# Attention with an expert layer on one core: three pieces of work moved in the expert part's written order

## The chip, the cores and the metric

The kernel runs on one core of a Trainium2 chip. The metric is device time of one execution, in microseconds (us), lower is better. The engines are called as in the profile: PE (TensorE products; PEld its weight loads), DVE (VectorE), ACT (ScalarE), POOL (GpSimd), SP (SyncE, which issues transfers); SPq and POOLq are their queues.

## The reference, cut to what matters

```python
# attention: 8 batches x 8 heads, 576 positions, 64 wide, block-causal (blocks of 64)
scores = q @ k.T / 8, masked where the key's block is later than the query's
attn = softmax(scores);  out = attn @ v          # x = out as [4608 rows, 512]
# expert layer: 8 experts, each row goes to one of them
logits = x @ w_gate + modality_bias[modality_id]
e = argmax(logits);  gate = softmax(logits)[e]
for each expert e, for its rows:  h = relu(x @ w1[e])          # 512 -> 1024
                                  out = gate * (h @ w2[e])     # 1024 -> 512
```

## The kernel before, in words

**Attention.** 32 pairs of heads go through a pipeline of slots, one pair per slot. The order of all work within a slot is a list written by hand (`ORDER`; `LAST` for the last slot, 32), and the program order on each engine is that order. `EARLY_STEPS` hangs first steps of the expert layer at places in slots 30 and 31: `ids` loads row numbers, `fetch` gathers 128 rows twice by POOL, `stage` lets SP load a weight chunk (512 KB) into one of two buffers `raw`, `cast00` to `cast02` let POOL's queue load the first three chunks rounded to the PE's format, and `lowerp` makes on POOL what the rounding left over (`L897`, chunk minus rounded chunk) and stages the next chunk. In each slot `vh` splits the values of a pair: ACT rounds (`L262`) and POOL subtracts (`L263`, tile `vhl`); the products `X`, `Y`, `W` of that pair (`L422`) need both.

**Routing.** After the last batch its rows' places are worked out (`routing`), POOL scatters row numbers into five blocks of `idlist` in memory (`L576`), and every expert's rows are then found there as a run of numbers.

**Experts.** `run_all` works through segments of rows in a fixed order: three of 256 rows for the fullest expert "a" (`n` is the segment's number; `n` = 0 is begun in the attention's last slot), three of 512 for "a" (`n` = 3 to 5), four of 512 for the second expert "b", one of 256 for a third expert "c" chosen on the chip, and a last one of 128 for "b" (`parts` = 1). What is left after these would run in a loop that tests its count on the chip. A segment of 256 rows takes: four up products (`up`, 24 products each, `L1007`) into one of three banks `s`, each followed by ACT's relu (`L1013`) and DVE's remainder (`L1014`); the next segment's rows brought into columns (`plain_rows`, ACT `L952`, and `turn_rows`, PE `L991`; or, for gathered quarters, `flip_rows`, DVE `L959`, and `split_rows`, `L969`, `L970`); and two halves of down products (`down`, 24 each, `L1053`), each given out by ACT's scaling (`L1086`) and a scatter of POOL (`L1087`). Segments from `n` = 3 on are gathered in quarters of rows, 16 gathers (`L940`) for 512 rows, eight of them issued in `n` = 1 and eight in `n` = 2. The numbers of the quarters come from `spread`: ACT multiplies row numbers by four (`L918`, tile `plain`), DVE copies and adds (`L920`, `L922`, tile `sub`). `load_ids` (`L909`, `L910`) reads a row out of a register's tile and lets POOL load that run of `idlist`; `next_segment` (DVE, 11 small instructions from `L1098`) chooses the third segment's expert, `trips` (to `L1112`) counts what is left. The last segment's up products (`up_few`, 24 products `L1029`) write `scratch` after relu (ACT `L1031`, DVE `L1033`); `turn_few` transposes that (`L1040`) and splits it (ACT `L1042`, DVE `L1043`).

Ahead of the loop over segments stand, in this order:

```python
idsa = self.load_ids(sel["rr"], 0, COVER - LEAD, "a")
idsb = self.load_ids(sel["rb"], 0, COVER_B, "b")
suba = self.spread(idsa, "a")
self.next_segment("c")
...
subb, subc = self.spread(idsb, "b"), self.spread(idsc, "c")
```

Of the kernel before, what the change touches and what calls it, by code (L numbers as in the profile page):

```python
# [14 lines left out]
I32 = mybir.dt.int32  # L15
AF = mybir.ActivationFunctionType
ALU = mybir.AluOpType
AX = mybir.AxisListType
ET = mybir.EngineType
# [4 lines left out]
N, DM, NE, DF = 4608, 512, 8, 1024  # L24
NPAIR = B * H // 2
PPB = H // 2
XW = 512
Z = 4
IW = 16
SLOT = 256  # L30
NSLOT = 9
FEW = 128
REGION = N + SLOT
NROW = NE * REGION
# [38 lines left out]

EARLY_STEPS = {
    (NPAIR - 2, "SA2"): ("stage", "ids", "cast00"),
    (NPAIR - 2, "ZB"): ("fetch", "stage", "cast01", "cast02", "lowerp"),
    (NPAIR - 1, "q1"): ("lowerp", "lowerp"),
    (NPAIR - 1, "ZB"): ("fetch",),
}
# [712 lines left out]
class Experts:  # L792
# [110 lines left out]
        self.nc.scalar.copy(self.target(k, name, c)[0], st)  # L903
        self.lower(on_pool)

    def load_ids(self, rowi, first, n, name, eng=ET.Pool, most=(NE - 1) * REGION):
        nc = self.nc
        ids = self.cst.tile([128, n // 128, 2], I32, name=f"ids_{name}")
        r = nc.values_load(rowi[0:1, 0:1], engines={eng}, min_val=0, max_val=most, skip_runtime_bounds_check_because="a row of an expert's own region")  # L909
        (nc.sync if eng == ET.SP else nc.gpsimd).dma_start(ids, self.idlist[bass.ds(r + first, n), 0:2].rearrange("(p a) o -> p a o", p=128))  # L910
        return ids

    def spread(self, ids, name):
        nc, n = self.nc, ids.shape[1]
        plain = self.cst.tile([128, n], F32, name=f"plain_{name}")
        lines = self.cst.tile([32, n, Z], F32, name=f"lines_{name}")
        sub = self.cst.tile([128, n, Z], I32, name=f"sub_{name}")
        nc.scalar.mul(plain, ids[:, :, 0], float(Z))  # L918
        for g in range(Z):
            nc.vector.tensor_copy(lines[:, :, g], plain[32 * g : 32 * g + 32])  # L920
        for z in range(Z):
            nc.vector.tensor_scalar(sub[32 * z : 32 * z + 32], lines, float(z), None, ALU.add)  # L922
        return sub

    def fetch(self, ids, t, name, nrows=N, parts=2, sub=None):
        s = Pair()
# [92 lines left out]
        self.up_relu(s)  # L1019

    def up_few(self, s):
        nc = self.nc
        wh, wl = self.w[s.name, 0]
        for f in range(2):
            fs = slice(512 * f, 512 * f + 512)
            hp = self.bank("s")
            mm = [(x, kc, w) for kc in range(4) for x, w in ((s.xh, wh), (s.xh, wl), (s.xl, wh))]
            for i, (x, kc, w) in enumerate(mm):
                nc.tensor.matmul(hp, self.x(x, kc, 128), w[:, kc, fs], start=i == 0, stop=i == len(mm) - 1)  # L1029
            if f == 0:  # L1030
                nc.scalar.activation(self.scratch[:, fs], hp, AF.Relu)  # L1031
            else:
                nc.vector.tensor_scalar(self.scratch[:, fs], hp, 0.0, None, ALU.max)  # L1033

    def turn_few(self, s, f):
        nc = self.nc
        x = self.bank("s")
        for a in range(4):
            m = 128 * (4 * f + a)
            nc.tensor.transpose(x[:, 128 * a : 128 * a + 128], self.scratch[:, m : m + 128], self.idf)  # L1040
        hh, hl = (t.rearrange("p a t -> p (a t)") for t in self.next_hidden())
        nc.scalar.copy(hh, x)  # L1042
        nc.vector.tensor_tensor(hl, x, hh, ALU.subtract)  # L1043
        s.hs += [(hh[:, 128 * a : 128 * a + 128], hl[:, 128 * a : 128 * a + 128]) for a in range(4)]
# [70 lines left out]
    def run_all(self, steps):  # L1115
        tc, ctx, nc, cst, sel, plan = self.tc, self.ctx, self.nc, self.cst, self.sel, self.plan
        dve = nc.vector
        self.wk = wk = ctx.enter_context(tc.tile_pool(name="wk", bufs=1, side="right", reuse_waits="tile"))
        self.w["b", 0] = [wk.tile([128, 4, DF], F32R, name=f"w0{x}b") for x in "hl"]
        w2 = [wk.tile([128, 2, DM], F32R, name=f"w1b{i}") for i in range(5)]  # L1120
        self.xl = [wk.tile([128, 512], F32R, name=f"xl{i}") for i in range(3)] + [self.xlast]
        self.o1 = self.ps_o.tile([128, 512], F32, name="o1")
        sb = [self.ps_s.tile([128, 512], F32, name="s") for _ in range(3)]
        self.sb, self.tb = sb, [self.ps_t.tile([128, 512], F32, name="t") for _ in range(2)]
        self.ys = [self.o0, self.o1, self.bbank, sb[2]]
        self.w["b", 1] = [w2[0:4], w2[4:5] + self.low2]
        s = self.parts[0]
        flat = self.xg[1]
        self.parts.append(self.fetch(*plan[2]))
        self.down(s, 0, range(6))  # L1130
        for f in steps[0:13]:
            f()
        self.down(s, 1, range(6))
        for f in steps[13:]:
            f()
        self.flush()
        for i in range(2):
            self.down(s, i, range(6, 8))
        self.rem, left = (cst.tile([128, NE], F32, name=n) for n in ("rem", "left"))
        self.rowc, self.expc = (cst.tile([128, 1], I32, name=n) for n in ("rowc", "expc"))  # L1140
        idsa = self.load_ids(sel["rr"], 0, COVER - LEAD, "a")
        idsb = self.load_ids(sel["rb"], 0, COVER_B, "b")
        suba = self.spread(idsa, "a")
        self.next_segment("c")
        sel["ec"] = self.expc
        idsc = self.load_ids(self.rowc, 0, SLOT, "c", most=NROW - SLOT)
        dve.tensor_tensor(left, self.run, sel["start"], ALU.subtract)
        self.more = self.trips(left)
        subb, subc = self.spread(idsb, "b"), self.spread(idsc, "c")

        wide = (COVER - LEAD) // 512
        plan += [(idsa, 4 * t, "a", N, 4, suba) for t in range(wide)]
        plan += [(idsb, 4 * t, "b", N, 4, subb) for t in range(COVER_B // 512)]
        plan += [(idsc, 0, "a", N, 2, subc), (idsb, 2 * NSLOT - 2, "b", N, 1, subb)]
        segs = self.parts + [self.fetch(*x) for x in plan[NLEAD:]] + [None]
        for n in range(1, len(plan)):
            s, nxt = segs[n : n + 2]
            ahead = segs[max(n + 1, NLEAD)]

            def follow(part):  # L1160
                if nxt is None:
                    return
                if nxt.sub is not None:
                    self.split_rows(nxt, part)
                elif part == 0:
                    self.turn_rows(nxt)

            if s.parts == 4:
                self.sb = sb[0:2]
                for m in range(8):  # L1170
                    self.up_wide(s, m)
                    self.give_owed()
                    if m > 1:
                        self.down_wide(s, m - 2)
                    self.gather(ahead, 3)
                    if m in (2, 5) and self.staged:
                        self.convert(n < NLEAD + wide)
                    if m == 6:
                        self.flip_rows(nxt)
                follow(0)  # L1180
                self.down_wide(s, 6)
                follow(1)
                self.down_wide(s, 7)
            else:
                if s.parts == 1:
                    self.up_few(s)
                    self.turn_few(s, 0)
                    self.turn_few(s, 1)
                    self.hturn += 2
                else:  # L1190
                    for m2 in range(4):
                        self.up(s, m2)
                        self.give_owed()
                        self.gather(ahead, 2)
                        if m2 == 1 and n < NLEAD:
                            self.convert(True)
                        if m2 == 2 and nxt.sub is None:
                            self.plain_rows(nxt, flat)
                if nxt and nxt.sub is not None:
                    self.flip_rows(nxt)  # L1200
                follow(0)
                self.down(s, 0)
                follow(1)
                if s.parts == 2:
                    self.down(s, 1)
        assert not self.staged and not self.owed

# [95 lines left out]
```

## Time and profile before

| | us |
|---|---|
| median of three runs (lowest, highest) | 832.88 (831.9, 835.57) |
| the profiled execution | 832.91 |
| its span, first to last instruction | 831.3 |
| PE busy in the span | 801.5 (96%) |
| DVE, ACT, POOL busy | 466.1, 465.3, 550.6 |
| mean granted PE clock | 0.984 of full speed |

A busy share of 96% is a mean over stages. What PE still waits for, and where its clock is not the full one, says what can be had; the rows below are read for that. The profiled execution's time lies 1.6 us over its span and 0.03 us over the median.

### The profile page before, as it was taken

The page shows a single profiled execution, that of the slowest core. Times are in us where ns is not written, and L with a number is a line of the kernel's source. Part 1 is how long each engine was busy: PE and PEld are TensorE (multiplying, and loading weights), DVE is VectorE, ACT ScalarE, POOL GpSimd, SP SyncE. Part 2 cuts the span into 40 slices and gives each one's busy share as a digit, 9 for nine tenths or more (in the row PEclk, how much of TensorE's full clock was granted, in tenths as well). Part 3 has the DMA queues.
Part 4 walks back from the last instruction along what each step waited for, and adds up shares of the span by engine and source line. Part 5 has one row for each costly group of instructions (what it writes and reads, how often), then busy time and mean ns, then how long its engine had stood idle before and what let it go on. Part 6 is the DMA issues. An engine that isn't in the chain of part 4 may idle for free.

```text
span 831.3 us, 15373 instructions
## 1 busy us (share of the span) xinstructions
PE 801.5 (96%) x5027; PEld 717.7 (86%) x5027; DVE 466.1 (56%) x1695; ACT 465.3 (56%) x1384; POOL 550.6 (66%) x399
## 2 busy tenths in 40 slices
PE   7999999999999999998949999999999999999995
PEld 5999999999999999998948888888888888888884
DVE  5889999999999999995631313131223213231220
ACT  6999999999999998996412312222131313222221
POOL 6998789898999999968355572655645362714030
PEclk9999999999999999999988999999999999999998
DMA  8887877767786768676611221221222131211010
GB/s 256 244 259 214 243 214 223 234 190 237 213 266 189 241 184 271 185 201 174 230 32 61 77 76 39 75 76 70 82 85 67 47 104 42 85 51 42 21 51 22
DMA packets 64306, 117.91 MB, mean 142 GB/s; under 512 B 18761, under 2 KB 31929, under 8 KB 64216
## 3 DMA queue, kind: packets, MB, share of 16 engines
q1 hardware_dynamic: 53600, 96.00, 38.6%
q0 software_dynamic: 10624, 20.89, 7.9%
q8 instruction: 41, 0.67, 0.3%
q14 instruction: 41, 0.34, 0.1%
HBM read 77.21 MB, written 21.95 MB: 119 GB/s over the span
## 4 chain that ended last, share of the span: by engine, by line
PE 40%; issue 34%; POOL 16%; DVE 4%; DMA 3%; ACT 1%; POOLq 1%; SPq 0%; DVEq 0%
PE o L422 11%; POOL xr L940 11%; PE b L441 6%; PE s L286 5%; PE s L287 4%; PE t L345 3%; POOL out L1087 3%; PE t L350 2%; PE s L278 2%; PE t L331 1%; PE t L363 1%; DVE scratch L291 1%; PE s L279 1%; DMA xrows<-xr 1%; DVE ptl L382 1%
## 5 line engine op out<-in xcount | busy, mean ns | idle before, releaser
L382 DVE TENSOR_TENSOR ptl<-t,pth 128x512 fp32r<-128x512 f32 (+3 forms) x288 | 140.1, 505 | 16.4 <-ACT pth L375 14.0
L291 DVE TENSOR_SCALAR_CACHE_REDUCE scratch<-s 128x128 bf16<-128x128 f32 (+4 forms) x288 | 132.6, 478 | 9.2 <-PE s L287 6.4
L319 ACT ACTIVATE pm<-s,nm 128x256 f32<-128x256 f32 (+3 forms) x256 | 134.8, 535 | 5.2 <-DVE scratch L291 4.6
L375 ACT CAST pth<-t 128x512 fp32r<-128x512 f32 (+3 forms) x288 | 122.8, 453 | 16.1 <-PE t L345 10.7
L422 PE MATMUL o<-pth,vhl 128*128 128x320 f32 (+3 forms) x384 | 110.6, 306 | 2.7 <-POOL vhl L263 2.5
L422 PE MATMUL o<-ptl,vhl 128*128 128x320 f32 (+3 forms) x384 | 110.8, 308 | 0.0
L286 PE MATMUL s<-qkt 128*128 128x256 f32 (+3 forms) x256 | 89.9, 364 | 1.4 <-DVE qkt L238 1.4
L215 POOL TENSOR_TENSOR qkt<-rawq,qkt 64x1280 fp32r<-64x1280 f32 x30 | 87.7, 2925 | 2.4
L211 POOL TENSOR_TENSOR z<-raw,qkt 64x1152 fp32r<-64x1152 f32 x30 | 79.8, 2659 | 13.3 <-issue 8.3
L940 POOL DMA_INDIRECT xr<-xrows,sub_b x68 | 69.8, 1027 | 20.6 <-issue 20.3
L1087 POOL DMA_INDIRECT out<-scratch,ids_b x17 | 17.0, 1002 | 98.8 <-ACT scratch L1086 84.5
L287 PE MATMUL s<-z 68*128 68x256 f32 (+3 forms) x256 | 80.0, 325 | 1.2 <-DMA z<-cm 1.2
L422 PEld LDWEIGHTS o<-pth,vhl 128*128 128x128 f32 x384 | 73.1, 190 | 4.7 <-POOL vhl L263 2.8
L1065 ACT ACTIVATE qkt<-s 128x512 fp32r<-128x512 f32 x28 | 16.8, 599 | 103.8 <-PE s L1063 103.8
L1065 ACT ACTIVATE ptl<-s 128x512 fp32r<-128x512 f32 x28 | 16.8, 599 | 102.8 <-PE s L1063 102.8
L422 PEld LDWEIGHTS o<-ptl,vhl 128*128 128x128 f32 x384 | 73.2, 191 | 1.3
L441 PE MATMUL b<-bk,ot 128*128 128x72 f32 x512 | 64.7, 269 | 0.5 <-DVE ei_a L97 0.3
L441 PEld LDWEIGHTS b<-bk,ot 128*128 128x128 f32 x512 | 64.2, 192 | 0.9 <-ACT ott L434 0.9
L1066 DVE SCALAR_TENSOR_TENSOR qkt<-s,qkt 128x512 fp32r<-128x512 f32 x14 | 9.7, 692 | 86.9 <-ACT qkt L1065 86.9
L940 POOL DMA_INDIRECT xr<-xrows,sub_a x48 | 48.3, 1006 | 14.0 <-issue 13.4
L319 ACT ACTIVATION_READ_ACCUMULATOR pm<-s,nm 128x1 f32 x256 | 53.2, 208 | 0.0
L286 PEld LDWEIGHTS s<-qkt 128*128 128x128 f32 x256 | 49.2, 192 | 2.5 <-DVE qkt L238 1.6
(372 smaller groups left out, 2210.5 us busy)
## 6 DMA issues: line engine op xcount, KB each, us to landing
raw<-qk SPq DMA_DIRECT2D x30, 640.0 KB, 4.3
rawq<-qk SPq DMA_DIRECT2D x30, 640.0 KB, 5.0
raw<-w SPq DMA_DIRECT2D x23, 512.0 KB, 3.5
vrt<-vr SPq DMA_DIRECT2D x32, 320.0 KB, 5.2
k2t<-z SPq DMA_DIRECT2D x64, 144.0 KB, 4.8
xrows<-xr SPq DMA_DIRECT2D x8, 1024.0 KB, 8.9
z<-qkt SPq DMA_DIRECT2D x30, 256.0 KB, 5.3
idlist<-xr SPq DMA_DIRECT2D x8, 304.0 KB, 4.1
```

The lines of the kernel that those rows point to most:

```text
L211: pool.tensor_tensor(d.k2[0:64], k, d.k[0:64], ALU.subtract)
L215: pool.tensor_tensor(d.q[0:64], q, d.q[0:64], ALU.subtract)
L286: pe.matmul(o, d.q[:, h, qs], d.k[:, h, 0:n], start=True, stop=False)
L287: pe.matmul(o, d.q2[0:68, h, qs], d.k2[0:68, h, 0:n], start=False, stop=True)
L291: dve.tensor_scalar(jks[jturn[0] % 4][:, 0 : s.shape[-1]], s, -SCALE, start, ALU.mult, ALU.min, accum_out=o)
L319: act.activation(d.pm[h][:, CHUNK_OFF[c] : CHUNK_OFF[c] + n], s[:, 256 * i : 256 * i + n], AF.Exp, bias=d.nm[:, h, c : c + 1], scale=SCALE ...
L375: act.copy(dst[0], s)
L382: dve.tensor_tensor(dst[1], s, dst[0], ALU.subtract)
L422: pe.matmul(o, w, r, start=part != "W" and i == 0, stop=part != "Y" and i == len(mm) - 1)
L441: pe.matmul(d.b[h][:, 72 * c : 72 * c + 72], d.ot[h][:, 128 * c : 128 * c + 128], w, start=True, stop=True)
L940: s.gathers.append(lambda to=to, at=at: gather(to, None, quarters, bass.IndirectOffsetOnAxis(ap=at, axis=0), bounds_check=Z * nrows - 1, o ...
L1087: last = nc.gpsimd.indirect_dma_start(self.out, bass.IndirectOffsetOnAxis(ap=s.ids[:, s.t + i, 0:1], axis=0), yo, None, bounds_check=N - 1 ...
```

## The change

Three things move; no instruction's size changes.

- At the end of slot 30 the remainder of the first weight chunk (`lowerp`) and the second `stage` stand ahead of the two gathers and the two rounding loads.
- `spread` of "a" and "b" and "c", and the choice of the third segment with its load (`third`), are taken out of the place ahead of the loop and put behind up products of `n` = 1 and `n` = 2 (`chores`); in `n` = 1 the gathers behind the four up products are 0, 2, 3, 3 instead of 2 each.
- The last segment's up products stand between the fourth and fifth of eight steps of the second down half of segment "c", and their relu goes to the row buffer `rows[1]` instead of `scratch`.

```diff
-    (NPAIR - 2, "ZB"): ("fetch", "stage", "cast01", "cast02", "lowerp"),
+    (NPAIR - 2, "ZB"): ("stage", "lowerp", "fetch", "cast01", "cast02"),
...
-        nc = self.nc
+        nc, wide = self.nc, self.rows[1]
...
             if f == 0:
-                nc.scalar.activation(self.scratch[:, fs], hp, AF.Relu)
+                nc.scalar.activation(wide[:, fs], hp, AF.Relu)
             else:
-                nc.vector.tensor_scalar(self.scratch[:, fs], hp, 0.0, None, ALU.max)
+                nc.vector.tensor_scalar(wide[:, fs], hp, 0.0, None, ALU.max)
...
-        suba = self.spread(idsa, "a")
-        self.next_segment("c")
-        sel["ec"] = self.expc
-        idsc = self.load_ids(self.rowc, 0, SLOT, "c", most=NROW - SLOT)
-        dve.tensor_tensor(left, self.run, sel["start"], ALU.subtract)
-        self.more = self.trips(left)
-        subb, subc = self.spread(idsb, "b"), self.spread(idsc, "c")
+        def third():
+            self.next_segment("c")
+            sel["ec"] = self.expc
+            self.load_ids(self.rowc, 0, SLOT, "c", most=NROW - SLOT, ids=idsc)
+            dve.tensor_tensor(left, self.run, sel["start"], ALU.subtract)
+            self.more = self.trips(left)
+        chores = {
+            (1, 1): lambda: self.spread(idsa, suba, "a"),
+            (1, 3): third,
+            (2, 0): lambda: self.spread(idsb, subb, "b"),
+            (2, 2): lambda: self.spread(idsc, subc, "c"),
+        }
...
-                    self.up_few(s)
                     self.turn_few(s, 0)
                     self.turn_few(s, 1)
...
                         self.give_owed()
-                        self.gather(ahead, 2)
+                        chores.get((n, m2), lambda: None)()
+                        self.gather(ahead, (0, 2, 3, 3)[m2] if n == 1 else 2)
...
-                if s.parts == 2:
+                if nxt and nxt.parts == 1:
+                    self.down(s, 1, range(4))
+                    self.up_few(nxt)
+                    self.down(s, 1, range(4, 8))
+                elif s.parts == 2:
                     self.down(s, 1)
```

In the rows of the program order below, lines of the changed kernel are mostly one lower than before (`L1013` is `L1012`).

On POOL at the end of slot 30 (`qkt_110` is the first weight chunk, `xr_114` the gathered rows, `vhl` the last pair's values), before:

```order
L263 TENSOR_TENSOR vhl<-vrt,vhl 128x10x64
L936 DMA xr_114<-xrows,ids_lead 128x512 x2
L892 ISA
L892 DMA qkt_108<-w 128x4x256
L892 ISA
L892 DMA z_102<-w 128x4x256
L897 TENSOR_TENSOR qkt_110<-raw_111,qkt_110 128x1024
L263 TENSOR_TENSOR vhl<-vrt,vhl 128x10x64
```

and now, where the remainder `L897` has gone from just ahead of the second `vhl` to just ahead of the gathers:

```order
L263 TENSOR_TENSOR vhl<-vrt,vhl 128x10x64
L897 TENSOR_TENSOR qkt_110<-raw_111,qkt_110 128x1024
L935 DMA xr_114<-xrows,ids_lead 128x512 x2
L892 ISA
L892 DMA qkt_108<-w 128x4x256
L892 ISA
L892 DMA z_102<-w 128x4x256
L263 TENSOR_TENSOR vhl<-vrt,vhl 128x10x64
```

On ACT at the start of `n` = 1 (the scalings of `n` = 0, then this segment's relus), before:

```order
L1086 ACTIVATE scratch<-o_6861,ids_lead 128x512
L918 ACTIVATE plain_a<-ids_a 128x12
L918 ACTIVATE plain_b<-ids_b 128x17
L918 ACTIVATE plain_c<-ids_c 128x2
L1013 ACTIVATE qkt_110<-s 128x512
L1013 ACTIVATE qkt_109<-s 128x512
L903 CAST w0hb<-raw_112 128x4x256
L1013 ACTIVATE ptl_104<-s 128x512
L952 COPY xr_114<-xr_114 128x512 x2
L1013 ACTIVATE ptl_104<-s 128x512
```

and now, with two relus ahead of `plain_a`, and `plain_b` and `plain_c` gone to `n` = 2:

```order
L1085 ACTIVATE scratch<-o_6861,ids_lead 128x512
L1012 ACTIVATE qkt_110<-s 128x512
L1012 ACTIVATE qkt_109<-s 128x512
L918 ACTIVATE plain_a<-ids_a 128x12
L903 CAST w0hb<-raw_112 128x4x256
L1012 ACTIVATE ptl_104<-s 128x512
L951 COPY xr_114<-xr_114 128x512 x2
L1012 ACTIVATE ptl_104<-s 128x512
```

On ACT at the end of the kernel (segment "c" given out, then the last segment), now; before, the relu `L1031` stood behind both scalings of `ids_c`:

```order
L1085 ACTIVATE scratch<-o_98,ids_c 128x512
L1030 ACTIVATE xr_115<-s 128x512
L1085 ACTIVATE scratch<-o_6861,ids_c 128x512
L1041 CAST qkt_110<-s 128x512
L1041 CAST qkt_109<-s 128x512
L1085 ACTIVATE scratch<-o_98,ids_b 128x512
```

The second scaling of "c" now stands directly ahead of the last segment's first cast.

## Rows read from the trace of the kernel before

**Rows 1.** PE's waits over the span: who waited <- for whom: us, times, longest.
```profile
PE s L1007 <- DVE qkt L1014: 11.8, 1, 11.8
PE o L422 <- POOL vhl L263: 2.5, 1, 2.5
PE s L1040 <- DVE scratch L1033: 0.4, 1, 0.4
```

**Rows 2.** Timeline around n = 1: start, us, engine, line [idle before <- releaser].
```profile
416.92 5.91 PE L1007 MATMUL s<-z,qkt 128*128 128x256 f32 x48
...
424.85 1.08 POOL L910 DMA_DIRECT2D ids_a<-idlist  x1
...
428.15 0.21 ACT L918 ACTIVATE plain_a<-ids_a 128x12 f32<-128x12 int32 x1 [10.34 <-DMA ids_a<-idlist]
...
429.14 0.75 DVE L922 TENSOR_SCALAR sub_a<-lines_a 32x48 int32<-32x48 f32 x4
...
432.70 0.15 DVE L1112 CAST counti<-count 128x1 int32<-128x1 f32 x1
...
433.75 1.08 POOL L940 DMA_INDIRECT xr<-xrows,sub_a  x1 [0.30 <-DVE lines_b L920]
...
435.89 1.04 ACT L903 CAST w0hb<-raw 128x1024 fp32r<-128x1024 f32 x1
...
437.31 1.15 ACT L952 COPY xr<-xr 128x512 f32<-128x512 f32 x2
...
437.46 5.35 PE L1007 MATMUL s<-z,qkt 128*128 128x256 f32 x24 [11.75 <-DVE qkt L1014]
```

**Rows 3.** Windows, PE alone: stretch, us, busy, granted clock, DMA share, GB/s.
```profile
384.00:385.00 1.00, 0.85 (x5) 0.74 0.93 236
387.00:388.00 1.00, 1.00 (x6) 0.55 0.04 8
...
428.00:429.00 1.00, 0.00 (x0) 0.93 0.53 17
...
442.00:443.00 1.00, 1.00 (x9) 0.75 0.50 120
```

**Rows 4.** Timelines of POOL, ACT and PE at the end of the attention.
```profile
376.18 1.10 POOL L936 DMA_INDIRECT xr<-xrows,ids_lead  x1 [8.03 <-DVE scratch L291]
...
380.16 2.44 POOL L897 TENSOR_TENSOR qkt<-raw,qkt 128x1024 fp32r<-128x1024 f32 x1
...
382.09 1.17 ACT L952 COPY pm<-xr 128x512 f32<-128x512 f32 x2
...
382.47 1.62 POOL L263 TENSOR_TENSOR vhl<-vrt,vhl 128x640 fp32r<-128x640 f32 x1
...
384.14 0.39 PE L422 MATMUL o<-pth,vhl 128*128 128x256 f32 x1 [2.52 <-POOL vhl L263]
...
384.80 1.08 PE L991 MATMUL t<-cf,pm 128*128 128x128 f32 x4
...
388.36 0.88 PE L1007 MATMUL s<-z,qkt 128*128 128x256 f32 x6
```

**Rows 5.** Chain (start, us, what), 375 to 475; then landings of chunk loads, 364 to 384.
```profile
368.37 6.91 DMA xrows<-xr
...
DMA to landing us min/median/max: 4.6/5.2/5.8
```

**Rows 6.** Timelines of POOL, DVE and PE from the last gather of n = 2 to n = 3.
```profile
468.63 1.00 POOL L940 DMA_INDIRECT xr<-xrows,sub_a  x1 [0.30 <-issue]
...
472.78 1.29 DVE L970 TENSOR_TENSOR xl<-xr,z 128x512 fp32r<-128x512 f32 x2 [0.73 <-ACT z L969]
...
476.98 0.39 PE L1063 MATMUL s<-z,qkt 128*128 128x512 f32 x1
```

**Rows 7.** Timeline of the last segment.
```profile
809.95 0.69 ACT L1086 ACTIVATE scratch<-o,ids_c 128x512 f32<-128x512 f32 x1 [4.85 <-PE o L1053]
...
815.30 0.60 PE L1040 MATMUL s<-cf,scratch 128*128 128x128 f32 x4
```

More of the change, by code (lines that the diff above doesn't have):

```diff
@@ L904, in convert, with load_ids @@
         self.lower(on_pool)
-    def load_ids(self, rowi, first, n, name, eng=ET.Pool, most=(NE - 1) * REGION):
+    def load_ids(self, rowi, first, n, name, eng=ET.Pool, most=(NE - 1) * REGION, ids=None):
         nc = self.nc
-        ids = self.cst.tile([128, n // 128, 2], I32, name=f"ids_{name}")
+        if ids is None:
+            ids = self.cst.tile([128, n // 128, 2], I32, name=f"ids_{name}")
         r = nc.values_load(rowi[0:1, 0:1], engines={eng}, min_val=0, max_val=most, skip_runtime_bounds_check_because="a row of an expert's own region")
@@ L911, in load_ids, with spread @@
         return ids
-    def spread(self, ids, name):
+    def spread(self, ids, sub, name):
         nc, n = self.nc, ids.shape[1]
@@ L916, in spread @@
         lines = self.cst.tile([32, n, Z], F32, name=f"lines_{name}")
-        sub = self.cst.tile([128, n, Z], I32, name=f"sub_{name}")
         nc.scalar.mul(plain, ids[:, :, 0], float(Z))
@@ L922, in spread @@
             nc.vector.tensor_scalar(sub[32 * z : 32 * z + 32], lines, float(z), None, ALU.add)
-        return sub
     def fetch(self, ids, t, name, nrows=N, parts=2, sub=None):
@@ L1039, in turn_few @@
             m = 128 * (4 * f + a)
-            nc.tensor.transpose(x[:, 128 * a : 128 * a + 128], self.scratch[:, m : m + 128], self.idf)
+            nc.tensor.transpose(x[:, 128 * a : 128 * a + 128], self.rows[1][:, m : m + 128], self.idf)
         hh, hl = (t.rearrange("p a t -> p (a t)") for t in self.next_hidden())
@@ L1142, in run_all @@
         idsb = self.load_ids(sel["rb"], 0, COVER_B, "b")
-        suba = self.spread(idsa, "a")
-        self.next_segment("c")
-        sel["ec"] = self.expc
-        idsc = self.load_ids(self.rowc, 0, SLOT, "c", most=NROW - SLOT)
-        dve.tensor_tensor(left, self.run, sel["start"], ALU.subtract)
-        self.more = self.trips(left)
-        subb, subc = self.spread(idsb, "b"), self.spread(idsc, "c")
+        idsc = cst.tile([128, SLOT // 128, 2], I32, name="ids_c")
+        suba, subb, subc = (cst.tile([128, x.shape[1], Z], I32, name=f"sub_{n}") for x, n in ((idsa, "a"), (idsb, "b"), (idsc, "c")))
+        def third():
[10 more added lines that the diff above has]
+        }
         wide = (COVER - LEAD) // 512
```

## The prediction

> **What bounds the kernel now.** I read the waits of PE first, since the page's busy shares say that PE works nearly all the time. Over the span PE has two waits that count and one small one [rows 1]: 11.8 us for DVE's remainder of an up product, 2.5 us for POOL's `vhl`, 0.4 us in the last segment. Everything else in the expert part is PE behind PE, so time moves only where one of these waits moves, where PE's clock moves, or where a new wait opens.
>
> Then the timeline around the long wait [rows 2]. PE runs three groups of up products of `n` = 1 (each half of 5.91, so 2.95 us) and stops at 425.71, because the fourth needs a bank that ACT and DVE have not emptied. They have not, since ahead of the relus in ACT's order stands the multiplication of `ids_a`, and that load lands only at 428.15 (issued at 424.85). Behind it DVE works through spreads and the third segment's choice until 432.85, and ACT meets `plain_c`, before a relu is reached. PE goes on at 437.46, and then with a group of 24 products in 5.35 us instead of 2.95.
>
> [...]
>
> Last the end of the attention [rows 4]. POOL stands for 8.03 us until 376.18, then gathers, starts two rounding loads, makes the remainder (2.44 us from 380.16), and only then `vhl`, for which PE waits until 384.14.
>
> **First part: remainder ahead of the gathers.** What the gathers wait for is the store of the same buffer, 6.91 us from 368.37 [rows 5], so the wait stays. The remainder needs its rounding load, which takes at most 5.8 us to land [rows 5]. It is issued ahead of the slot's own `vhl` of 1.6 us, which ended when POOL went idle at 368.15, so by 366.6, and is there by 372.4. Then the remainder runs until about 374.9, inside the 8.03 us in which POOL has nothing to do. Gathers keep their time, `vhl` starts 2.44 us earlier and ends near 381.7, when PE arrives. PE is next late for the plain copies of the gathered rows: ACT ends them at 383.26 (382.09 + 1.17, [rows 4]), and PE's transposes, at 384.80 before, can start at 383.3. From there to the first up group took 3.56 us (to 388.36), 3.1 of them at half clock; with two waits below 1 us the clock should stay, so 2.0. That makes 385.3, a gain of 3.0 us. But later chunks' loads hang on POOL's remainders, which move by 2.44 only. I take 2.6. Bounds: 0 if the remainder isn't covered, 3.1 if nothing later holds. Of the transfers moved, the next chunk's load is issued near 375 instead of 382.6, in front of the gathers; were they delayed by it, the plain copies would be, and PE one for one.
>
> **Second part: the chores.** Now two relus precede the wait for `ids_a`, so the fourth up group finds its bank empty and PE runs until 428.66 (425.71 + 2.95). Queued behind the wait on ACT are the weight cast, the third relu, the copies of the next segment's rows and the fourth relu; PE's next work, the transposes, needs the copies. From the cast's start to the copies' end took 2.57 us (435.89 to 438.46, [rows 2]); put behind `plain_a` (428.15 + 0.21) that is 430.93. So PE waits 2.3 us where it waited 11.75. On DVE the two remaining low halves queue behind the spread, which ends at 429.9; they are needed at the down products, behind the transposes. The third choice and count took from 429.9 to 432.85, 2.95 us, and run after the fourth low half, until about 435; behind them stand the next segment's low rows, needed only by the first up group of `n` = 2, 48 down products on. They are covered, and so are the later spreads, four copies and four additions each, between up groups of 2.95 us.
>
> Whether the clock falls for a wait of 2.3 us the trace doesn't say outright: it fell for 2.52, and in the last tenths of a microsecond of it PE was already at work [rows 3, 4]. I take a fall, at 1.7 us. Before: 11.75 + (5.35 - 2.95) = 14.15. After: 2.3 + 1.7 = 4.0. Gain 10.15 us, with 8.5 as the lower bound (the copies 1 us later, and a slow stretch that costs 2.4 as in the long wait) and 11.85 as the upper (no fall).
>
> [...] The sum would be 1.7 us smaller in time without the fall.
>
> POOL has to keep up, since PE comes to `n` = 3 ten us sooner. Sixteen gathers (1.30 us each with the 0.30 between, [rows 6]), two remainders (2.44), one id load (1.08, [rows 2]) and two scatters at the gathers' cost are 16 x 1.3 + 4.9 + 1.1 + 2.6 = 29.4 us from 429.9, when `sub_a` is ready. That ends near 459.5, or 460.2 with a wait for the second scaling: the last gather starts near 458.9. Before, the first pair of rows for `n` = 3 was ready 4.8 us after the last gather's start (472.78 + 0.65 against 468.63) and PE wanted it at 476.98, 3.5 us later. Now it is ready at 463.7; PE, 10.15 us sooner, wants it at 466.8. The slack stays at 3 us; a delay of POOL costs nothing up to there.
>
> [...] The spreads now stand among the gathers. [...]
>
> **Third part: the last up products.** PE's 24 products move, none goes. What they could gain is the 0.41 us that the transposes waited for DVE's relu [rows 1]. Against that, the second scaling of "c", 0.69 us, now stands on ACT between the last product and the cast of the transposed rows, while the transposes take 0.60 [rows 7]. The cast starts up to 0.69 later, at best not at all; I take 0.3 us lost. PE's first down products need that cast and DVE's part behind it, so the 0.41 is not regained. Bounds -0.4 and +0.7.
>
> **Sum.** Against the profiled time, 832.91, which is the median but for 0.03: - 2.6 - 10.15 + 0.3 = 820.5 us, 1.5% faster.
>
> **Rivals.**
> No slow stretch in `n` = 1: 820.5 - 1.7 = 818.8. For it, the wait is shorter than any for which the trace shows a fall; against it, how near the 2.52 lies.
> The first part pays nothing: the rounding load lands later than 373.7 (376.18 less 2.44), or the copies are late behind the earlier chunk. 823.1. Against it, 5.8 us as the longest landing.
> [...]
> The wait only changes its place, and the kernel is slower: ACT stands for `ids_a` inside `n` = 1, and everything for PE's transposes is behind it. If the load landed X us later than 428.15, PE would wait X more; from X = 12.4 the kernel is no faster, and at 17 it is 4.6 us slower, 837.5. The load took 3.3 us, and nothing in its neighbourhood takes five times that.
> The change doesn't do what it says in its third part: that is in the sum.
>
> **How the numbers follow.** Likeliest, 820.5: 0.46. No slow stretch, 818.8: 0.22. First part nothing, 823.1: 0.14. POOL at `n` = 3, 822.5: 0.09. Several of these losses with another slow stretch, 825 to 829: 0.07. The ids late: 0.02. The runs before spread from 1 us below to 2.7 above their median, so the range is 817 to 826, which leaves out the last two cases and little else. A measurement of this kernel can tell about 0.5%, 4.2 us, from no change: faster means below 828.7. All but the last two cases lie below; of the last but one most does. Faster 0.94, same 0.04, slower 0.02.
>
> **What would show it.** Of PE's waits the 11.8 us for DVE's remainder goes, and one of 2 to 2.6 us for ACT's copies `L951` comes, near 426 of the new span. The clock falls there for about 3.4 us, or not at all. PE's wait for `vhl` shrinks below 0.3 us, a wait of 0.5 to 1 us for the plain copies follows it, the remainder of the first chunk runs near 373, and no slow stretch follows. From `n` = 2 to the last segment PE has no wait over 0.5 us. In the last segment the first cast starts after the second scaling of "c". The prediction is wrong if PE waits at `n` = 3 for `xl`, if `ids_a` lands over 4 us after its issue, or if the POOL wait of 8 us moves to the remainder.

## The result and the profile after

| | before | after |
|---|---|---|
| median, us (lowest, highest; 4 runs each) | 834.23 (831.9, 836.78) | 821.07 (819.87, 822.0) |
| ratio, 95% interval | | 0.9841 [0.9805, 0.9877] |
| the profiled execution, us | 832.91 | 822.0 |
| its span, us | 831.3 | 820.3 |
| mean granted PE clock | 0.984 | 0.998 |

The kernel became 1.6% faster; forecast were 820.5 us and 1.5%. The time alone does not tell that forecast from three of its rivals: the interval, taken on 834.23 us, runs from 818.0 to 824.0 us, and 818.8, 822.5 and 823.1 lie in it too. The profiles have to tell. A ratio on record is not the quotient of the two medians, so that the two can give differences almost a microsecond apart; where it matters, the text says which is meant. Ratios are of the fast executions alone, which leaves out one of the twelve of the kernel with two remainders ahead: it took 1580.55 us, and why stays open.

Read as before, first PE's waits over the span after the change (who waited <- for whom: us, times, longest):

```profile
PE t L990 <- ACT xr L951: 2.0, 2, 1.8
...
PE s L287 <- DMA z<-qkt: 1.0, 2, 0.8
PE t L990 <- ACT pm L951: 0.7, 2, 0.5
...
PE o L1052 <- ACT qkt L1041: 0.4, 1, 0.4
```

The 11.8 and 2.5 us of [rows 1] are gone. The first row is what is left of the long wait, the third what lay under the short one. The second, for a transfer, is in the attention and has no counterpart in the profile before.

The timelines around `n` = 1 after the change (start, us, engine, line), against [rows 2]:

```profile
417.58 5.91 PE L1006 MATMUL s<-z,qkt 128*128 128x256 f32 x48
...
425.51 1.08 POOL L911 DMA_DIRECT2D ids_a<-idlist  x1
...
426.21 3.04 PE L1006 MATMUL s<-z,qkt 128*128 128x256 f32 x24
...
428.89 0.21 ACT L918 ACTIVATE plain_a<-ids_a 128x12 f32<-128x12 int32 x1 [4.76 <-DMA ids_a<-idlist]
...
430.43 1.12 ACT L951 COPY xr<-xr 128x512 f32<-128x512 f32 x2
...
431.09 0.33 PE L990 MATMUL t<-cf,xr 128*128 128x128 f32 x1 [1.84 <-ACT xr L951]
431.61 0.98 PE L990 MATMUL t<-cf,xr 128*128 128x128 f32 x7 [0.19 <-ACT xr L951]
```

The fourth up group runs on at 426.21, PE stops behind it, and the transposes start as soon as the first of ACT's two copies is done. The windows (us, busy of each engine, then PE's clock, DMA share, GB/s) show a full clock at both places where [rows 3] show a fall (in the profile before to 0.50 of full from 385 to 387 and from 429 to 442):

```profile
428.00:436.00 8.00, 5.97 (x35) 4.92 (x34) 5.95 (x12) 4.24 (x8) 4.61 (x4) 1.00 0.13 21
384.00:388.00 4.00, 3.27 (x26) 2.75 (x26) 2.53 (x9) 3.36 (x11) 3.50 (x4) 1.00 1.02 259
```

The end of the attention after the change, against [rows 4]:

```profile
375.61 2.39 POOL L897 TENSOR_TENSOR qkt<-raw,qkt 128x1024 fp32r<-128x1024 f32 x1 [3.00 <-DMA qkt<-w]
379.60 1.10 POOL L935 DMA_INDIRECT xr<-xrows,ids_lead  x1 [1.60 <-DVE scratch L291]
...
383.58 1.62 POOL L263 TENSOR_TENSOR vhl<-vrt,vhl 128x640 fp32r<-128x640 f32 x1
...
385.03 0.27 PE L364 MATMUL t<-cf,pm 128*128 128x128 f32 x1
385.25 0.39 PE L422 MATMUL o<-pth,vhl 128*128 128x256 f32 x1
...
386.47 0.33 PE L990 MATMUL t<-cf,pm 128*128 128x128 f32 x1 [0.54 <-ACT pm L951]
...
389.02 1.24 PE L1006 MATMUL s<-z,qkt 128*128 128x256 f32 x9
```

The remainder fills the gap ahead of the gathers, `vhl` ends at 385.20 as PE comes, and PE then waits for ACT's plain copies. The last segment, against [rows 7]:

```profile
804.18 1.04 PE L1039 MATMUL s<-cf,xr 128*128 128x128 f32 x8
...
804.43 0.69 ACT L1085 ACTIVATE scratch<-o,ids_c 128x512 f32<-128x512 f32 x1 [5.00 <-PE o L1052]
805.02 1.06 ACT L1041 CAST qkt<-s 128x512 fp32r<-128x512 f32 x2
...
805.65 2.15 PE L1052 MATMUL o<-w1b,qkt 128*128 128x512 f32 x7 [0.43 <-ACT qkt L1041]
```

The wait for DVE's relu has become one for ACT's cast, which stands behind the scaling.

**Where the time went.** I cut both spans at rows that PE executes in either kernel. From the end of the last transposes ahead of the `vhl` products (`L364`) to the first up product of `n` = 0, "stretch A": 381.62 to 388.36 before, 385.30 (385.03 + 0.27) to 389.02 after, so 6.74 and 3.72. From the first up product of `n` = 1 to that of `n` = 2, "stretch B": 37.70 before and 25.91 after (417.58 to 443.49). The first products of `n` = 2, before and after:

```profile
454.62 0.28 PE L1007 MATMUL s<-z,qkt 128*128 128x256 f32 x1
```

```profile
443.49 0.28 PE L1006 MATMUL s<-z,qkt 128*128 128x256 f32 x1
```

Between A and B both profiles take 28.56, and behind B ("stretch C") 376.68 and 376.81 to the end. Sum: -3.02 - 11.79 + 0.13 = -14.7. The span fell by 11.0 only, since everything ahead of A took 3.68 us longer. Nothing in the change stands there that could do that: in the thirteen profiles of this study that part ends anywhere from 381.45 to 387.72, and 381.45 belongs to a kernel with the whole change (the early spread, below).

### The profile page after: what moved, and what is told of

It is laid out like the page before. It is cut to its first block, busy times and chain, and to the rows that moved or that the text cites. A ratio compares the mean times of both kernels' runs of the same rounds, so it can differ in the third digit from the quotient of the medians.

```text
span 820.3 us, 15372 instructions
## 1 busy us (share of the span) xinstructions
PE 802.3 (98%) x5027; PEld 717.2 (87%) x5027; DVE 470.8 (57%) x1695; ACT 465.1 (57%) x1384; POOL 551.8 (67%) x399
## 4 chain that ended last, share of the span: by engine, by line
PE 37%; issue 34%; POOL 19%; DMA 6%; DVE 3%; ACT 1%; POOLq 1%; SPq 0%; ACTq 0%
PE o L422 11%; POOL xr L939 11%; PE b L441 5%; PE s L286 4%; PE s L287 4%; POOL out L1086 3%; PE t L345 3%; PE t L350 2%; DMA z<-qkt 2%; PE s L278 2%; PE t L331 1%; PE t L363 1%; DMA raw<-w 1%; PE s L279 1%; DMA rawq<-qk 1%
## 5 line engine op out<-in xcount | busy, mean ns | idle before, releaser
L287 PEld LDWEIGHTS s<-z 68*128 68x128 f32 x256 | 49.9, 195 | 3.2 <-issue 1.5
```

The costliest lines, as they stand in the source:

```text
L287: pe.matmul(o, d.q2[0:68, h, qs], d.k2[0:68, h, 0:n], start=False, stop=True)
```

## The experiments

The first four ran on one chip, on which the kernel before takes 842.85 us (median of 7); the next four on a second one (832.44, 9 runs); the last three on a third (835.73, 17 runs). Ratios are to the kernel before on the same chip.

**The choice and the spreads alone** (second part of the change).

```diff
-        suba = self.spread(idsa, "a")
-        self.next_segment("c")
...
+            (1, 1): lambda: self.spread(idsa, suba, "a"),
+            (1, 3): third,
+            (2, 0): lambda: self.spread(idsb, subb, "b"),
+            (2, 2): lambda: self.spread(idsc, subc, "c"),
```

> Only the spreads, the third segment's choice and the gathers' shares are moved. Three stretches of PE's timeline are compared, since whole times of unchanged code differ by some us between executions: A, from the end of the transposes ahead of the vhl wait to the first up product of the expert layer (6.74 us before, 3.72 changed); B, from the first up product of n = 1 to that of n = 2 (37.70 before, 25.91 changed); C, from there to the last instruction (376.7 before, 376.8 changed). Theory: the parts are separate, so A stays at 6.7 with its slow clock, B is 25.9, C 376.7, and the time falls by 11.8 us. Rival: B's clock stays up only because the first part spared the slow stretch 40 us earlier; then B is 27 to 28 with a fall of the clock, and the time falls by about 10.

Measured: 832.18 us, ratio 0.9877 [0.9858, 0.9896], by which 10.4 us of 842.85 are gained (10.7 between the medians). Stretch B is 25.98, with PE's wait for the copies 1.43 + 0.19 and no slow products behind it: the seven down products that follow take 1.88 us, as after the change, where the clock is 1.00. Stretch A is 3.99, although the first part of the change is missing. Why, PE's timeline shows:

```profile
364.34 0.30 PE L422 MATMUL o<-p,vhl 128*128 128x64 f32 x1 [1.26 <-DMA p<-p4l]
...
385.25 0.39 PE L422 MATMUL o<-pth,vhl 128*128 128x256 f32 x1 [1.20 <-POOL vhl L263]
```

PE had lost 1.26 us twenty microseconds earlier to a late transfer of `p4l` (32 KB, which SP's queue copies from one tile of the pair to another); POOL did not lose it, so `vhl` was that much nearer when PE came for it. The rival, that B's clock stays up only because a slow stretch in A is spared, was not put to the test, since A has none here either.

**The remainder ahead of the gathers alone** (first part).

```diff
-    (NPAIR - 2, "ZB"): ("fetch", "stage", "cast01", "cast02", "lowerp"),
+    (NPAIR - 2, "ZB"): ("stage", "lowerp", "fetch", "cast01", "cast02"),
```

> Only the remainder of the first chunk and a stage are moved ahead of the gathers. Theory: A is 3.7 us, B and C are as before (37.7 with the long wait, 376.7), and the time falls by 3.0 us. Rival: the gain is swallowed further on, since loads of later chunks move by 2.4 us only; then the stretch from the first up product to the first of n = 1 grows from 28.56 us, and the time falls by less than 2.5.

Measured: 840.74 us, ratio 0.9984 [0.9963, 1.0006]: 1.3 us by the ratio, 2.1 between the medians, not told from nothing, where the prediction had 2.6 and the expectation 3.0. In its profile the wait for `vhl` is gone and A is 3.73. So the mechanism works and the time gains less; the next runs bear on why. The sign of the rival, a longer stretch between A and B, is there as well: 30.98 instead of 28.56. But 1.93 of the 2.42 are idle time in `L1007` that the profile gives to nothing ("issue"), and the two profiles of the changed kernel, with the same order on POOL, take 28.56. So nothing shows that the remainder swallows its gain further on.

**The last up products alone** (third part; one execution).

```diff
-                    self.up_few(s)
...
+                if nxt and nxt.parts == 1:
+                    self.down(s, 1, range(4))
+                    self.up_few(nxt)
+                    self.down(s, 1, range(4, 8))
```

> Only the last segment's up products are moved into the down products of the segment ahead, and write the row buffer. Theory: PE's wait of 0.4 us goes from one place to another, and from the last product ahead of the transposes to the first down product it is 1.70 us as in the changed kernel, against 1.66 before; A and B are as before. Rival: the second scaling on ACT costs its whole 0.7 us.

Measured: 842.54 us beside 842.85. From the start of the first transposes to the first down product behind them it took 1.46 (824.23 to 825.69), 1.42 in the kernel before (815.30 to 816.72) and 1.47 after the change: 0.05 us lost, not the rival's 0.7. Its profile is worth more for the other place. PE's timeline and PE's clock (us, busy, granted clock, DMA share, GB/s):

```profile
364.79 0.30 PE L422 MATMUL o<-p,vhl 128*128 128x64 f32 x1 [1.63 <-DMA p<-p4l]
...
388.89 0.33 PE L991 MATMUL t<-cf,pm 128*128 128x128 f32 x1 [0.76 <-ACT pm L952]
```

```profile
368.00:370.00 2.00, 2.00 (x11) 0.50 0.78 219
```

Here the late transfer was followed by a granted clock of 0.50 in each of three windows from 366 to 372; PE came so late that there was no wait for `vhl` at all (A 3.72), without the first part of the change.

**The first spread and its gathers in the last step of `n` = 1.**

```diff
-            (1, 1): lambda: self.spread(idsa, suba, "a"),
-            (1, 3): third,
+            (1, 3): lambda: (self.spread(idsa, suba, "a"), self.gather(segs[NLEAD], 4), third()),
...
-                        self.gather(ahead, (0, 2, 3, 3)[m2] if n == 1 else 2)
+                        self.gather(ahead, (0, 0, 0, 4)[m2] if n == 1 else 2)
```

> The changed kernel, with the spread of a moved from behind the second up group of n = 1 to behind the fourth, and all eight gathers of n = 1 behind it. Theory: PE waits in n = 1 because the copies of the next segment's rows stand behind ACT's wait for ids_a; with that wait behind them B loses the rest of its wait and is 23.9 us, and POOL, some 1.5 us later with its gathers, still has the sixteen ready in time, so the time is 2.0 us below the changed kernel's. DVE's first instruction of the third choice, which took 3.1 us while POOL made a remainder, takes 0.2 again, since that remainder is then over. Rival: POOL's gathers become late and PE waits at n = 3 for as much as it gains; B 23.9 but C above 378.

Measured: 831.03 us, ratio 0.986 [0.9843, 0.9878]. The wait for the copies in `n` = 1 is gone, and B is 24.33. On this chip, though, PE shows waits in the expert part that the profile gives to nothing ("issue"): 7.1 us in all here, 6.6 us in the run of the remainder alone, whose largest row is

```profile
PE s L1076 <- issue: 3.1, 3, 1.2
```

They lie in up products, most of them in segments that no edit touches, so on this chip 1.5 us could not be told. Nor does the rival's sign say anything here: C is 389.69, over its 378, but 385.42 with the choice and the spreads alone on this chip. PE shows no wait for rows at `n` = 3.

**The changed kernel again**, beside the next three.

> The changed kernel as it is, so that the next three have it beside them on one chip. The parts run alone gave 0.988 (choice and rows later) and 0.998 (remainder first) of the kernel before; if parts add up, this gives 0.984 to 0.987. Theory: 11.8 us less between the first products of n=1 and of n=2, and 3.0 us less between the end of attention's last transposes and the first up product in executions in which the kernel before waits 2.5 us there. Rival: the second saving is a thing of one execution; then the ratio is 0.986 to 0.988.

Measured: 819.78 us (818.51 to 823.36), ratio 0.9854 [0.9827, 0.988]; A 3.72, B 25.86, no "issue" wait. The interval holds both forecasts.

**The changed kernel with the remainder behind the gathers again** (the first diff above, reversed).

> The changed kernel with the remainder behind the gathers again, as before. Theory (the wait for vhl is there in every execution): 2.5 to 3.0 us slower than the changed kernel, with PE's wait of 2.5 us on vhl back in the profile. Rival (the wait is there only where PE comes early; where it waits elsewhere first, 1.3 or 1.6 us for a late p4l transfer in two profiles, POOL has caught up): 0 to 1.5 us slower in the median, and a profile with a late p4l transfer shows no wait for vhl or one of about 1 us.

Measured: 820.82 us, ratio 0.986 [0.9837, 0.9883]: 1.0 us slower between the medians, not told from nothing, and in the rival's 0 to 1.5. PE's timeline:

```profile
363.34 0.30 PE L422 MATMUL o<-p,vhl 128*128 128x64 f32 x1 [0.96 <-DMA p<-p4l]
...
383.97 0.39 PE L422 MATMUL o<-pth,vhl 128*128 128x256 f32 x1 [0.92 <-POOL vhl L263]
```

A is 3.73: a wait of 0.92 for `vhl` costs nothing, since under it lies the one for the plain copies (0.76 + 0.19 in the run beside it). The second thing to see is PE's clock behind the wait in `n` = 1. First this run, whose wait there is 1.78, then the changed kernel again, with 1.79:

```profile
430.00:431.00 1.00, 1.00 (x5) 0.50 0.28 78
431.00:432.00 1.00, 1.00 (x4) 0.50 0.27 70
432.00:433.00 1.00, 1.00 (x4) 0.50 0.01 0
```

```profile
430.00:431.00 1.00, 1.00 (x7) 1.00 0.32 78
431.00:432.00 1.00, 1.00 (x6) 1.00 0.26 66
432.00:433.00 1.00, 1.00 (x6) 1.00 0.02 4
```

The same stretch of code behind the same wait, in two kernels that differ only at the end of the attention, runs at 0.50 of the full clock in one execution and at 1.00 in the other; B is 27.43 against 25.86, so the slow stretch costs 1.57. In neither is there a slow stretch in A, so a spared one does not keep B's clock up.

**The first spread one up group earlier.**

```diff
-            (1, 1): lambda: self.spread(idsa, suba, "a"),
+            (1, 0): lambda: self.spread(idsa, suba, "a"),
```

> The changed kernel with the first spread one step earlier, behind the first up product group of n=1 instead of the second, so that ScalarE waits for ids_a with two eviction copies behind it instead of one. Theory (the wait is for the landing of ids_a, 428.9 in the profile, and only what is queued behind it counts): PE stops at about 426 for 3 to 4 us instead of 2.0 at 429 to 431, so 1 to 2 us slower than the changed kernel. If a wait of this length makes the clock fall, as 2.52 us did in the kernel before, 1.7 us more: 2.7 to 3.7 us slower. Rival (the slack of PE behind that place takes it up): no difference.

Measured: 820.42 us, ratio 0.9859 [0.9834, 0.9884]. PE did not stop for 3 to 4 us at 426. The first relu still stands ahead of the spread, and its bank is the one that the fourth group takes; so the wait stays at the transposes, longer by the one relu more behind `ids_a` (0.47 from start to start):

```profile
427.67 0.33 PE L990 MATMUL t<-cf,xr 128*128 128x128 f32 x1 [2.26 <-ACT xr L951]
```

In that profile the clock fell behind it (0.57 of full from 428 to 432), and B is 27.91, of which 2.05 over 25.86 are 0.47 of wait and 1.6 of slow clock. The median moved by 0.6 us, about as much as the wait and not told from nothing; the forecast of 1 to 2 us or more fell.

**Late spread, and the last transposes inside the segment ahead.** The late spread as above, and:

```diff
-                    self.turn_few(s, 0)
-                    self.turn_few(s, 1)
...
-                    self.down(s, 1, range(4, 8))
+                    self.down(s, 1, range(4, 6))
+                    self.turn_few(nxt, 0)
+                    self.turn_few(nxt, 1)
+                    self.down(s, 1, range(6, 8))
```

> The changed kernel with the first spread and its gathers in the last step of n=1, and the last segment's two sets of transposes inside the segment ahead, between its sixth and seventh group of down products. Theory: the 2.0 us wait in n=1 goes (1.5 us less there, as one profile showed) and the 0.4 us wait ahead of the last down products goes: 1.5 to 2 us faster than the changed kernel. Rival (gathers that start 2 us later make n=3 late, or POOL's work is only moved): no faster than the changed kernel, with a new wait of PE at the start of n=3.

Measured: 816.71 us (815.83 to 818.34), ratio 0.981 [0.9789, 0.9831], 3.1 us below the changed kernel beside it, where 1.5 to 2 were forecast; its slowest execution is faster than that one's fastest. From `n` = 0 on the profile has no wait of PE but 0.9 us for the plain copies; B is 23.44. The transposes run between down products:

```profile
427.98 1.03 PE L990 MATMUL t<-cf,xr 128*128 128x128 f32 x8
...
799.25 1.04 PE L1039 MATMUL s<-cf,xr 128*128 128x128 f32 x8
```

Between the two profiles B is shorter by 2.42, of which the wait was 1.98 (1.79 + 0.19), and C by 0.68. The gathers that start later did not make `n` = 3 late.

**A second remainder ahead of `vhl`** in the kernel before.

```diff
-    (NPAIR - 2, "ZB"): ("fetch", "stage", "cast01", "cast02", "lowerp"),
-    (NPAIR - 1, "q1"): ("lowerp", "lowerp"),
+    (NPAIR - 2, "ZB"): ("fetch", "stage", "cast01", "cast02", "lowerp", "lowerp"),
+    (NPAIR - 1, "q1"): ("lowerp",),
```

> The kernel before with a second of POOL's remainders ahead of vhl (in it one stands there), so that vhl comes 2.4 us later still. Theory: PE waits for it in every execution, and the wait grows from 2.5 to 4.9 us: 2.4 us slower than the kernel before, with the stretch from the last transposes of the attention to the first up product at 9.1 us or more (6.74 before, 3.7 where nothing waits). Rival (an earlier late p4l transfer takes the wait's place in some executions): the wait in the profile is 4.9 us less what PE stood for p4l, and the median grows by 1 to 2 us.

Measured: 839.98 us, ratio 1.0046 [1.0027, 1.0065]: 3.8 us slower by the ratio, 4.25 between the medians, where 2.4, or by the rival 1 to 2, were forecast. Stretch A is 10.30, with a mean granted clock of 0.91 from 388 to 424, behind the wait. POOL and PE:

```profile
385.88 2.34 POOL L897 TENSOR_TENSOR qkt<-raw,qkt 128x1024 fp32r<-128x1024 f32 x1 [1.61 <-DMA qkt<-w]
388.18 1.53 POOL L263 TENSOR_TENSOR vhl<-vrt,vhl 128x640 fp32r<-128x640 f32 x1
...
389.77 0.58 PE L422 MATMUL o<-pth,vhl 128*128 128x256 f32 x1 [5.42 <-POOL vhl L263]
```

The second remainder brought its own wait, 1.61 for its chunk, so `vhl` came 4.0 later and not 2.4. With the 1.35 that PE stood for `p4l` in this profile, 2.52 - 1.35 + 4.0 = 5.2, near the 5.42 seen. POOL's work ahead of `vhl` does pass on to PE one for one, less what PE was late.

**The first spread ahead of `n` = 1 again**, all else as changed.

```diff
+        self.spread(idsa, suba, "a")
         chores = {
-            (1, 1): lambda: self.spread(idsa, suba, "a"),
```

> The changed kernel with the first spread back in front of the up products of n=1, the third segment's choice and the other spreads still late. Theory (the wait of 11.8 us is the landing of ids_a, and behind it the choice and the later spreads in ScalarE's and VectorE's order): about 5 us of it come back, since ScalarE stands for ids_a with all relus behind it and VectorE makes the spread (1.5 us) before the first low half; with a slow stretch of 1.7 to 2.4 us the first products of n=2 come 30.5 to 31.2 us after those of n=1 (37.7 before, 25.9 or 27.4 changed). So 0.989 to 0.992 of the kernel before. Rival one (the landing of ids_a is all of it): 37 us, no gain but the remainder's. Rival two (the choice and its load are all of it): 26 us, as the changed kernel.

Measured: 825.43 us, ratio 0.9891 [0.9859, 0.9922]; B 30.12, a little under the 30.5 to 31.2 forecast. ACT and PE:

```profile
425.83 0.21 ACT L918 ACTIVATE plain_a<-ids_a 128x12 f32<-128x12 int32 x1 [10.32 <-DMA ids_a<-idlist]
...
428.35 4.62 PE L1006 MATMUL s<-z,qkt 128*128 128x256 f32 x24 [4.95 <-DVE qkt L1013]
```

The group of 24 takes 4.62 where it takes 3.04 at full clock (0.59 of full from 428 to 432). So 4.95 of the 11.75 us are the landing of `ids_a` and its spread ahead of the relus; the other 6.8 are the choice, its load and the later spreads. Both rivals fall.

**The third spread one group later**, in the kernel with late spread and turns (one execution).

```diff
-            (2, 2): lambda: self.spread(idsc, subc, "c"),
+            (2, 3): lambda: self.spread(idsc, subc, "c"),
```

> The kernel with the late first spread and early transposes, with the third spread one up group later, so that its four copies don't run beside POOL's remainder. If POOL's work on SBUF holds VectorE's instruction (1.75 and 1.91 us for four copies of 32 x 2 beside it, 0.67 before), they take 0.7 us again; if the place after a wait is the cause, they stay near 1.8. No change of the time is expected from either: 816 to 818 us on the chip that gave 816.7.

Measured: 823.63 us on the third chip, with 3.6 us of "issue" waits there; the forecast of 816 to 818 was for another chip, so the time says nothing about it. What it shows of DVE and POOL stands in the last section.

## Why the prediction was right, and where its terms were off

**The second part** was priced at 10.15 us: 14.15 before, 4.0 after, of which 1.7 were a slow stretch that was counted on. That figure is the work lost in the short fall of the profile before: 0.50 of the full clock from 385 to 387, with the shares of [rows 3] on both sides, makes 1.7 us. The falls seen behind the wait for the copies in `n` = 1 cost 1.57 and 1.6. Alone it measured 10.4 us by the ratio. Against the 37.70 of the profile before, single profiles give one of two numbers: 11.8 where the clock stays (25.91, 25.86, 25.98), 10.3 where it falls (27.43); the four profiles with the old order on ACT have B from 37.01 to 38.29, so either is good to about 1 us. The profile of the result shows the rival without a slow stretch, not the likeliest case. My doubt about a fall for 2.3 us has the answer "sometimes": the clock stayed behind stops of 1.43, 1.79 and 1.84 us and fell behind 1.78 and 2.26. With 1.79 on one side and 1.78 on the other, the length of the stop alone does not decide it; what does was not shown. The rest of the step held: ids landed 3.4 us after their issue, PE waited 1.84 + 0.19 where 2.3 stood, 0.27 less because I let PE wait for both copies and it starts after the first. The spread ahead of `n` = 1 gave back 4.95 us of wait, as the reading of ACT's order says.

**POOL** kept up as reckoned: from the first product of `n` = 1 to the last gather 42.0 us were forecast (416.92 to 458.9) and 41.1 seen (417.58 to 458.72); `n` = 3 began at 465.86 with no wait. The rival of a late `n` = 3 (822.5) fell: no run shows its 2 us of wait for rows, also none with gathers that start later still.

**The first part**, 2.6 us (3.0 worked out), is the term that was mis-sized as a term of the median. Against the profile it was made for it was exact: A fell by 3.02, the plain copies are the next wait, and no slow stretch follows. But the wait of 2.5 us that it removes is not in every execution. Four profiles have the old order of POOL, with this chain:

| profile | late `p4l` | wait for `vhl` | stretch A |
|---|---|---|---|
| kernel before | none | 2.52 | 6.74 |
| choice and spreads alone | 1.26 | 1.20 | 3.99 |
| without the remainder first | 0.96 | 0.92 | 3.73 |
| last up products alone | 1.63, then a slow clock | none | 3.72 |

Where PE comes late, the wait shrinks to 1.20, 0.92 or nothing; under it lies the 0.95 us of the plain copies, so its removal is worth 0.3 us or nothing. The times say 1.3 us alone (by the ratio, interval -0.5 to 3.1) and 1.0 with the rest (between the medians). The prediction took one execution's wait for every execution's. Of the five profiles with POOL's old order (the fifth has two remainders ahead) four have the late transfer, of the eight with the remainder first one; nothing that was moved stands ahead of it, so the count may be chance. That it is this that makes the gain smaller is in keeping with all profiles, but the differences in time are too small to show it. Why the transfer of `p4l` is late in some stays open: from its issue to its landing it takes 1.8 us in the kernel before and 3.4 in the one with late spread and turns. SP's issue behind it (`xrows`, twice) takes 2.0 to 2.6 us in those profiles and 1.29 in the others, and that last kernel has the remainder first.

**The third part**, 0.3 us lost, measured 0.05 at its place: the cast starts 0.84 behind the transposes' start (804.18 to 805.02), and 0.63 where no scaling stands between (799.25 to 799.88, with the turns inside the segment ahead), so it was held by 0.2 and not by up to 0.69. The wait is not regained, as forecast.

So the total is near (-13.2 us between the medians, -12.4 forecast) with the second part a little above and the first below its term. That these two misses cancel in part is luck, and so is where a single execution lies, as the ends of the attention, 381.45 to 387.72, show.

## What to carry to other kernels

An instruction that waits for a load belongs in an engine's order behind everything that is ready and that another engine is about to need; what it then still costs is what is queued behind it, and that can be moved once more, as the late spread did for another 2.4 us. Before a wait of one profile is priced as a gain, look for what else can make the waiting engine late on the way there: a wait that a late transfer sometimes hides is worth its mean, not its length. And ask what lies under the wait: here one of 0.92 us cost nothing, since 0.95 us for the plain copies lay under it.

## What the runs showed of the hardware

**DVE stood for POOL.** In the changed kernel a DVE subtraction of 8 columns, 0.17 us elsewhere, took 3.11 us and ended as POOL's remainder did. DVE and POOL there; then the kernel with late spread and turns, at four copies of 32 x 2; then the same copies one group later, beside a gather:

```profile
432.69 3.11 DVE L1097 TENSOR_TENSOR rem<-run,start 128x8 f32<-128x8 f32 x1
...
433.36 2.42 POOL L897 TENSOR_TENSOR w0lb<-raw,w0hb 128x1024 fp32r<-128x1024 f32 x1
```

```profile
449.84 3.31 DVE L920 COPY lines_c<-plain_c 32x2 f32<-32x2 f32 x4
...
450.19 2.42 POOL L897 TENSOR_TENSOR w0lb<-raw,w0hb 128x1024 fp32r<-128x1024 f32 x1
```

```profile
455.62 0.66 DVE L920 COPY lines_c<-plain_c 32x2 f32<-32x2 f32 x4
...
455.87 1.01 POOL L939 DMA_INDIRECT xr<-xrows,sub_a  x1 [0.31 <-issue]
```

So it is POOL's subtraction that holds DVE; beside the gather the copies took 0.66 us, 0.67 in the kernel before, and the gather 1.01 where 1.00 is usual. With the late spread the same DVE subtraction of 8 columns comes after POOL's (431.25, POOL done at 429.59) and takes 0.17 again, as had been expected of that run. Not every DVE instruction is held: in the changed kernel the remainder of an up product, which reads one tile and the bank `s`, takes its usual 0.69 inside POOL's subtraction.

```profile
452.22 2.41 POOL L897 TENSOR_TENSOR w0lb<-raw,w0hb 128x1024 fp32r<-128x1024 f32 x1
...
452.81 0.69 DVE L1013 SCALAR_TENSOR_TENSOR ptl<-s,ptl 128x512 fp32r<-128x512 f32 x1 [2.14 <-ACT ptl L1012]
```

In the first two pairs DVE stands until POOL is done: for 2.9 (3.11 - 0.17) and 2.6 us (3.31 - 0.66), ending at 435.80 where POOL ended at 435.78, and, for the one copy of the four that took 2.80 us (3.31 less three of 0.17), at 452.64 where POOL ended at 452.61. Beside POOL's subtraction at 452.22, too, one copy of `lines_c` took 1.24 us where 0.16 is usual, and ended at 454.66 where POOL ended at 454.63. By the records DVE began 0.67 and 0.35 us ahead of POOL in the first two pairs. By what means POOL's subtraction holds these DVE instructions, and why not the remainder of the up product, is not shown. POOL's gathers, among which the spreads stand, stayed within 0.1 us of their 1.00 (0.99 to 1.07 over the 48 of "a" in the changed kernel). DVE's standing cost no time here: among PE's waits in that kernel's expert part none is for DVE.

**Chips differ in more than the total.** On two of three chips PE had waits of 0.2 to 1.2 us in the expert part that the profile gives to no releaser, up to 7.1 us in a span; on the third, and in the first pair of profiles, none. Whatever they are, they come with the chip or the execution: a comparison of 1 us needs kernels side by side.
